# Longer DMA packets for all weights of an adaLN / cached-attention / MLP decode block, with the re-layout of the activations that they need

## The chip, the cores and the metric

The kernel runs on one core of a Trainium2 chip. Times are device microseconds (us) of one launch; a profiled execution also has a span, from its first to its last instruction, about 1.8 us shorter than the time of the same run. Engine names as in the profile: PE (TensorE), PEld (its weight loads), DVE (VectorE), ACT (ScalarE), POOL (GpSimd), SP (SyncE, which here only issues DMAs; SPq is its queue).

## The reference, cut to what matters

Two tokens (batch 2, one position each) go through one block. The weights and the caches are bf16.

```python
mod = (silu(c) @ w_mod).reshape(2, 6, 1, -1)            # w_mod 1024 x 6144
sa, ca, ga, sb, cb, gb = ...                            # its six parts
h = layernorm(x) * (1 + ca) + sa
q = h @ wq                                              # wq 1024 x 4096, 32 heads of 128
o = softmax(q k^T / sqrt(128)) v                        # caches 2 x 4 x 32768 x 128, 8 heads share one
x = x + ga * (o @ wo)                                   # wo 4096 x 1024
h = layernorm(x) * (1 + cb) + sb
x = x + gb * (gelu(layernorm(h) @ w1 + b1) @ w2 + b2)   # w1 1024 x 3584, w2 3584 x 1024
```

K and V are 134 MB, the weights 44 MB; every byte is used once. So the kernel is a long load from HBM, with everything else meant to hide under it.

## The kernel before

One ring of 160 KB per partition takes all loads. They are issued in the order of a list, each when the data that it overwrites has been used. One DMA moves 128 partitions; a run of bytes that is contiguous in HBM and in one partition becomes one packet of the profile's DMA records. What sets the packet length is therefore the layout of the source:

```python
wm_v = w_mod.rearrange("(p k) n -> p k n", k=KT8)
for k in range(KT8):                                    # 8 loads, one row of 12 KB per partition
    add(("wmod", k), [6 * DM], wm_v[:, k, :], k * 12 * KB)
for k in range(4):                                      # 2 rows of 8 KB per partition, from different places
    add(("wq", k), [2, HQ * D], A_wq[k * 256:(k + 1) * 256, :].rearrange("(k p) n -> p k n", p=128), (96 + 16 * k) * KB)
for i in range(NBG):                                    # 8 head pairs (batch x kv head)
    add_k(i, 0)                                         # 32 KB packets, ring bytes 0..32 KB
    add_k(i, 1)                                         # 32 KB packets, 32..64 KB
    add_v(i)                                            # 64 KB packets, 64..128 KB
# ... wo: 4 loads of 16 KB packets; w1: 4 loads, 7 KB; w2: 3 loads of 8 KB, then one of 6 KB, one of 2 KB
```

A matmul with such a weight contracts over the partitions, so the activation must lie on the partition on which the weight's row lies. With rows `(k p)`, partition p holds rows p, 128+p, ..., and the normed activation is already there (`inT`). One head pair is a body of the PE and DVE loop: K tiles are transposed by PE, evicted, multiplied with q; softmax; then P times V, after which V's space is free and SP issues V of the next pair.

The MLP's hidden row came out of w1 as rows, was copied to SBUF by ACT and DVE, turned to columns by 16 fp32 matmuls on PE, and got its bias on DVE.

## Time and profile before

| | before |
|---|---|
| time, median of the first 3 runs | 421.65 us (421.61 to 421.91) |
| span | 419.9 us |
| HBM read | 178.28 MB, 425 GB/s over the span |
| packets of the data queue | 8562 |
| first packet starts / last ends | 1.7 us / 416.2 us |
| PE busy / DVE / ACT | 68% / 40% / 38% |

The DMA view of the kernel before: mean busy share of the 16 DMA engines in 40 slices (tenths), what they moved, and packets, megabytes and the share of 16 engines' span that the packets took.

```profile
DMA  8999999999999999999999999999999999999995
GB/s 338 431 431 422 440 435 487 395 408 448 440 431 425 431 443 425 437 437 450 415 418 465 431 409 437 465 415 416 475 425 400 450 462 418 397 432 419 427 428 241
DMA packets 8573, 178.44 MB, mean 425 GB/s; under 512 B 873, under 2 KB 880, under 8 KB 2162
...
q1 hardware_dynamic: 8562, 178.28, 98.8%
```

Every slice but the first and the last is full. The same over stretches of the run (us of the stretch, busy us of each engine, granted PE clock, DMA share, GB/s):

```profile
0.00:4.00 4.00, 0.00 (x0) 0.00 (x0) 0.00 (x0) 1.28 (x1) 3.09 (x15) 1.00 0.59 197
4.00:60.00 56.00, 26.02 (x205) 11.34 (x205) 5.84 (x23) 2.86 (x5) 0.43 (x2) 0.90 1.02 435
60.00:345.00 285.00, 212.85 (x4307) 182.52 (x4308) 140.85 (x262) 138.17 (x232) 2.19 (x14) 0.85 1.00 433
345.00:412.00 67.00, 42.36 (x559) 27.68 (x556) 19.90 (x60) 17.02 (x32) 0.22 (x1) 0.72 1.00 425
```

The share is 1.0 from 4 us to 412 us: the kernel is bound by its DMA engines. The chain of waits gives PE half of the span, but PE only keeps pace; where the stages meet, it waits for the loads. The timeline of the kernel before (start, length, engine, line, operation, in brackets the idle time before it and what ended it):

```profile
62.96 0.82 PE L506 MATMUL psKT<-ident,K 128*128 128x128 bf16 x6 [6.37 <-DMA K<-in_A_k_cache_dram]
...
382.17 1.90 PE L616 MATMUL psS<-wo,atT 128*32 128x512 bf16 x16 [3.82 <-DMA wo<-in_A_wo_dram]
...
402.52 3.87 PE L665 MATMUL psM<-identf,S_sb 128*128 128x8 f32 x16 [1.30 <-DVE x1b L668]
...
414.06 2.88 PE L695 MATMUL psO<-gT,w 128*128 128x2 bf16 x96 [1.08 <-DMA w<-in_B_w_dram]
...
418.09 0.35 SPq L706 DMA_DIRECT2D out_dram<-c  x1
```

PE waits 6.4 us for the first K, 3.8 us for the last wo, and 1.1 us for w2 just before the end. L665 are the 16 fp32 matmuls that turn the MLP's rows to columns.

### The profile page before, as it was taken

The numbers are of one execution on the slowest core, as the hardware profiler recorded it, in microseconds if no ns is written. First come the engines' busy times: TensorE is split into PE (matmuls) and PEld (weight loads), VectorE is DVE, ScalarE is ACT, GpSimd is POOL, SyncE is SP. The second block draws the span as 40 slices with busy tenths as digits, with TensorE's granted clock in tenths as the row PEclk, the third lists the DMA queues.
The fourth block names the chain that finished last, engine by engine and source line by source line (L and its number), as shares of the span: only waits on it lengthen the run. The fifth ranks groups of instructions, "written<-read, shape, count | busy, mean of one in ns | idle before, by whom it ended". The sixth has DMA issues, their size and how long they took to land.

```text
span 419.9 us, 11452 instructions
## 1 busy us (share of the span) xinstructions
PE 285.4 (68%) x5171; PEld 225.2 (54%) x5171; DVE 167.3 (40%) x347; ACT 159.3 (38%) x269; POOL 5.9 (1%) x31
## 2 busy tenths in 40 slices
PE   1547429856892898489559928965894699264575
PEld 1105009842891497269429915962793299122244
DVE  1102006540772376157417714750674177121311
ACT  2000005552566165436526652644365166600020
POOL 3000000000000000000000000000000000000000
PEclk9999858965997799599879969985998699686566
DMA  8999999999999999999999999999999999999995
GB/s 338 431 431 422 440 435 487 395 408 448 440 431 425 431 443 425 437 437 450 415 418 465 431 409 437 465 415 416 475 425 400 450 462 418 397 432 419 427 428 241
DMA packets 8573, 178.44 MB, mean 425 GB/s; under 512 B 873, under 2 KB 880, under 8 KB 2162
## 3 DMA queue, kind: packets, MB, share of 16 engines
q1 hardware_dynamic: 8562, 178.28, 98.8%
q8 instruction: 8, 0.13, 0.1%
q14 instruction: 3, 0.02, 0.0%
HBM read 178.28 MB, written 0.00 MB: 425 GB/s over the span
## 4 chain that ended last, share of the span: by engine, by line
PE 50%; DMA 30%; ACT 11%; DVE 6%; issue 2%; SPq 1%; ACTq 0%
PE psKT L506 27%; PE psS L518 10%; DMA K<-in_A_k_cache_dram 10%; PE psO L548 9%; DMA wo<-in_A_wo_dram 9%; ACT E_sb L538 8%; DMA w<-in_B_w_dram 7%; DMA wmod<-in_w_mod_dram 4%; DVE msum L563 2%; ACT KT_sb L510 2%; DVE m1c L523 1%; ACT S_sb L522 1%; PE psM L556 1%; PE psM L534 1%; PE psM L568 1%
## 5 line engine op out<-in xcount | busy, mean ns | idle before, releaser
L506 PE MATMUL psKT<-ident,K 128*128 128x128 bf16 x2048 | 154.4, 221 | 8.0 <-DMA K<-in_A_k_cache_dram 6.4
L510 ACT ACTIVATE KT_sb<-psKT 128x1024 bf16<-128x1024 bf16 x96 | 97.7, 1025 | 127.2 <-PE psKT L506 127.2
L512 DVE COPY KT_sb<-psKT 128x1024 bf16<-128x1024 bf16 x160 | 106.2, 688 | 45.5 <-PE psKT L506 44.8
L506 PEld LDWEIGHTS psKT<-ident,K 128*128 128x128 bf16 x2048 | 118.7, 98 | 9.3 <-DMA K<-in_A_k_cache_dram 6.5
L518 PE MATMUL psS<-qcur,KT_sb 128*128 128x8 bf16 x2048 | 87.0, 167 | 0.7
L518 PEld LDWEIGHTS psS<-qcur,KT_sb 128*128 128x128 bf16 x2048 | 76.9, 96 | 1.8 <-ACT KT_sb L510 1.4
L548 PE MATMUL psO<-V,E_sb 128*32 128x512 bf16 x512 | 44.6, 526 | 0.0
L538 ACT ACTIVATE E_sb<-S_sb,negm 128x256 bf16<-128x256 f32 x64 | 32.5, 507 | 23.8 <-DVE negm L535 22.0
L556 PE MATMUL psM<-onesf,rsum 128*128 128x1 f32 x16 | 4.7, 362 | 45.4 <-DVE rsum L555 45.4
L548 PEld LDWEIGHTS psO<-V,E_sb 128*32 128x32 bf16 x512 | 16.9, 127 | 23.9 <-issue 19.5
L556 PEld LDWEIGHTS psM<-onesf,rsum 128*128 128x128 f32 x16 | 4.0, 310 | 46.1 <-DVE rsum L555 46.1
L523 DVE TENSOR_REDUCE m1c<-psS 128x8 f32<-128x512 f32 x32 | 22.2, 693 | 13.5 <-ACT S_sb L522 13.4
L522 ACT ACTIVATE S_sb<-psS 128x512 f32<-128x512 f32 x32 | 19.0, 593 | 7.7 <-PE psS L518 7.7
L561 DVE TENSOR_SCALAR msum<-psO,mk 128x128 f32<-128x128 f32 x8 | 2.8, 351 | 42.9 <-PE psO L548 42.9
L555 DVE COPY rsum<-rowsum 128x128 f32<-128x128 f32 x8 | 1.8, 226 | 41.5 <-ACT E_sb L538 41.5
L456 PE MATMUL psS<-wmod,inT 128*32 128x512 bf16 x64 | 8.4, 622 | 11.8 <-DMA wmod<-in_w_mod_dram 11.8
L568 PE MATMUL psM<-msum,hmat 128*128 128x128 f32 x16 | 3.9, 326 | 13.0 <-DVE msum L563 13.0
L477 PE MATMUL psS<-wq,inT 128*32 128x512 bf16 x64 | 7.0, 587 | 7.8 <-DMA wq<-in_A_wq_dram 6.8
L529 PE MATMUL psM<-identf,m 128*8 128x128 f32 x16 | 3.4, 296 | 13.1 <-DVE m L526 13.1
L538 ACT ACTIVATION_READ_ACCUMULATOR E_sb<-S_sb,negm 128x1 f32 x64 | 12.0, 187 | 0.0
L568 PEld LDWEIGHTS psM<-msum,hmat 128*128 128x128 f32 x16 | 2.4, 188 | 16.9 <-DVE msum L563 16.9
L427 ACT ACTIVATE stat<-stat 128x2 f32<-128x2 f32 x3 | 0.6, 204 | 28.2 <-DVE stat L426 28.2
(116 smaller groups left out, 133.3 us busy)
## 6 DMA issues: line engine op xcount, KB each, us to landing
K<-in_A_k_cache_dram SPq DMA_DIRECT2D x16, 4096.0 KB, 25.6
wmod<-in_w_mod_dram SPq DMA_DIRECT2D x8, 1536.0 KB, 16.3
wq<-in_A_wq_dram SPq DMA_DIRECT2D x4, 2048.0 KB, 37.8
wo<-in_A_wo_dram SPq DMA_DIRECT2D x4, 2048.0 KB, 34.1
w<-in_B_w_dram SPq DMA_DIRECT2D x4, 1792.0 KB, 28.9
w<-in_B_w_dram SPq DMA_DIRECT2D x3, 2048.0 KB, 30.2
w<-in_B_w_dram SPq DMA_DIRECT2D x1, 768.0 KB, 28.0
w<-in_B_w_dram SPq DMA_DIRECT2D x1, 256.0 KB, 23.8
```

The costliest lines, as they stand in the source:

```text
L456: pe(lambda e, w=it.view, k=k, ch=ch, n=n, q=q: e.matmul(bank[n][32 * q:32 * q + 32, :], lhsT=inT[:, k, :], rhs=w[:, ch * 512:(ch + 1) * 512],
L506: pe(lambda e, kq=kq, jj=jj, w=kt, t=t: e.transpose(psKT[kq][:, jj * 128:(jj + 1) * 128], w[:, t, :], ident[:, :]), reads=[it.reg, "ident" ...
L510: act(lambda e, src=src: e.activation(KT_sb[g8][:, :, :], src, ACT.Copy), reads=[f"psKT{kq}"], writes=[f"KT_sb{g8}"], sem=f"ev{cc}_{g8}")
L512: dve(lambda e, src=src: e.tensor_copy(KT_sb[g8][:, :, :], src), reads=[f"psKT{kq}"], writes=[f"KT_sb{g8}"], sem=f"ev{cc}_{g8}")
L518: pe(lambda e, t=t, jj=jj: e.matmul(ps[:, t * HPG:(t + 1) * HPG], lhsT=KT_sb[g8][:, jj, :], rhs=qcur[:, :], start=True, stop=True), reads= ...
L522: act(lambda e: e.activation(Sc, ps[:, :].rearrange("p (t h) -> p h t", h=HPG), ACT.Copy), reads=[preg], writes=[f"S_sb_{cc}"], sem=f"sc{cc}")
L523: dve(lambda e: e.tensor_reduce(m1c[:, :, cc], ps[:, :].rearrange("p (t h) -> p h t", h=HPG), AX.X, ALU.max), reads=[preg], writes=[f"m1c{ ...
L538: act(lambda e: e.activation(E_sb[:, :, h, :], S_sb[:, h, :].rearrange("p (u t) -> p u t", t=4), ACT.Exp, bias=negm[:, h:h + 1], scale=SCA ...
L548: pe(lambda e, t4=t4, tg=tg, q=q: e.matmul(psO[32 * q:32 * q + 32, :], lhsT=E_sb[:, tg // 4, :, :].rearrange("p h t -> p (h t)"), rhs=vt[: ...
L556: pe(lambda e: e.matmul(psM[:, 144:145], lhsT=rsum16.rearrange("p h e -> p (h e)"), rhs=onesf[:, 0:1], start=True, stop=True), reads=["one ...
L563: dve(lambda e, q=q: e.scalar_tensor_tensor(out=msum[:, :], in0=psO[:, q * 128:(q + 1) * 128], scalar=mk4[:, q:q + 1], in1=msum[:, :], op0 ...
L568: pe(lambda e: e.matmul(psM[:, 256:384], lhsT=hmat.rearrange("p h e -> p (h e)"), rhs=msum[:, :], start=True, stop=True), reads=["hmat", " ...
```

## The change

Fewer and longer packets for the weights: a packet has a cost of its own beside its bytes. Every weight is now cut as `(p k)`, each partition taking adjacent rows, and several rows go into one load: w_mod 2 loads of 48 KB packets (8 of 12 KB), wq 2 of 32 KB (4 of 8), wo 2 of 32 KB (4 of 16), w1 2 of 28 KB (4 of 7), w2 3 of 16 KB (8) and the same two short last loads.

The rows of wq and w1 now lie on other partitions, so the activation is moved there (`to_lines`: 8 small matmuls with a selection matrix, a multiply with a mask, a reduce). The layout of the attention's output follows wo's. The MLP's rows are turned by one DVE transpose of 32 x 32 blocks straight from PSUM; the bias enters as a first matmul.

```diff
-    for k in range(KT8):
-        add(("wmod", k), [6 * DM], wm_v[:, k, :], k * 12 * KB)
-    for k in range(4):
-        add(("wq", k), [2, HQ * D], A_wq[k * 256:(k + 1) * 256, :].rearrange("(k p) n -> p k n", p=128), (96 + 16 * k) * KB)
+    for m in range(2):
+        add(("wmod", m), [4, 6 * DM], wm_v[:, 4 * m:4 * m + 4, :], m * 48 * KB)
+    wq_v = A_wq.rearrange("(p k) n -> p k n", k=KT8)
+    for m in range(2):
+        add(("wq", m), [4, HQ * D], wq_v[:, 4 * m:4 * m + 4, :], (96 + 32 * m) * KB)
     ...
+    for m, (j0, j1, off) in enumerate(W2_ITEMS):
+        add(("w2", m), [j1 - j0, DM], w2_v[:, j0:j1, :], off * KB)
     ...
-    modulate(inT[:, :, 0:2], "inT", 0, 1)
+    modulate(hb[:, :, :], "hb", 0, 1)
+    def to_lines():
+        for k in range(KT8):
+            pe(lambda e, k=k: e.matmul(psM[:, 128 + 16 * k:144 + 16 * k], lhsT=rep[:, k, :, :].rearrange("p c u -> p (c u)"),
+                                       rhs=hb.rearrange("p k b -> p (k b)"), start=True, stop=True), ...)
+        dve(lambda e: e.tensor_tensor(pick ..., psM[:, 128:256] ..., mblk ..., ALU.mult), ...)
+        dve(red, reads=["pick"], writes=["inT"])          # reduce into inT
+    to_lines()
     ...
-    load_row("act", psS[1], "psS1", 1)
-    load_row("dve", psO, "psO", 2, 96)
-    for n, nq in ((0, 4), (1, 3)):                        # 16 fp32 matmuls, then + b1
-        ...
+    dve(lambda e: e.transpose(zrow.rearrange("p (g n c) -> p g n c", n=2, c=16), psZ[:, :, 0:448].rearrange("p n (c g) -> p g n c", g=FT)), ...)
```

## The prediction

> **What bounds it now.** The DMA engines, from the first packet to the last. The DMA view shows a mean busy share of about 1.0 in nearly every slice of the 419.9 us span. The queue's packet records: first packet at 1.7 us, last ends at 416.2 us, so 414.5 us; their durations sum to 414.5 us per engine (16 engines). No idle time is left. The chain of waits names PE for half the span, but the attention loop (about 38 us per head pair) only keeps pace with the queue and ends 8 us before the wo weights land (PE waits for the last wo load until 382.2 us). At the end PE waits for w2 at 414.1 us; about 3 us of work and the output follow the last packet.
>
> **What the change is worth.** Durations of packets in steady state, by size: 7 KB 272 ns, 8 KB 309, 12 KB 460, 16 KB 611, 32 KB 1213, 64 KB 2418. That is a line: 7.7 ns per packet plus bytes at 27.19 B/ns. The slope is the port rate in the Trainium skill, "DMA: Bandwidth & Descriptors", section "Where 436 GB/s comes from" (16 x 32 B x 850 MHz, 27.2 B/ns per engine); this trace agrees, so only the 7.7 ns can be saved. Estimate per engine from that line:
> - w_mod: 64 x 460 to 16 x 1815 ns, -0.39 us
> - wq: 64 x 309 to 16 x 1213, -0.37
> - wo: 32 x 611 to 16 x 1213, -0.14
> - w1: 64 x 272 to 16 x 1062, -0.41
> - w2: 48 x 309 to 24 x 611, -0.17; the two small last pieces stay.
>
> Sum -1.5 us, plus 12 fewer semaphore writes of 9 ns, -0.1. All of it is on the critical resource, as long as the queue never runs dry.
>
> **What it adds, off the path.**
> - c and x now queue behind 6.3 MB (14.5 us) instead of 1.6 MB: they land near 17.5 us instead of 6.8, PE starts w_mod near 21 us instead of 10. PE finishes the second half about 5 us after it lands (before 1.5); with the new turn to lines (about 1.5 us: 8 matmuls, a multiply, a reduce) q is ready near 59 us instead of 57, still before K lands near 62.
> - wo in two items: after the last lands PE has 32 matmuls, not 16 (+1.5 us; 16 took 1.9), plus the turn (+1.4): w1 starts near 396.5 instead of 394.4, needs about 6.6 us as before.
> - The MLP: two copies, 16 fp32 transposes (3.9 us) and the bias add go; one VectorE transpose of 896 columns takes their place, estimated 1.1 us from the 512-column PSUM copy (0.69 us). Activations are ready near 406 instead of 407.7.
> - Attention: only layouts of small tensors.
>
> **Prediction.** 421.65 - 1.6 = 420.05 us, range 419.0 to 421.6. Faster by over 2%: 0.01; within 2%: 0.97; slower by over 2%: 0.02.
>
> **What would show it.** Packet records: 48 KB near 1815 ns, 28 KB near 1062; sum per engine 413.0 us, last end near 414.7. Landing: K's first wait ends near 62.2 instead of 62.96. The wait of PE for w2 stays just before the end, about 1.5 us earlier. A wait for c to about 17.5 us.
>
> **What would make it wrong.** The queue running dry because a K or V load is issued late; long packets slower than the line, or their strides of 64 or 56 KB slower in HBM; the VectorE transpose taking over 4 us, or the w1 chain getting later than the last w2 piece; uneven last landings.

## The result, and the profile after

| | before | after |
|---|---|---|
| time, median of 4 runs | 421.75 us (421.61 to 421.91) | 421.61 us (421.37 to 423.05) |
| span of the profiled run | 419.9 us | 419.6 us |
| packets of the data queue | 8562 | 5428 |
| first packet starts / last ends | 1.7 / 416.2 us | 1.7 / 416.0 us |
| sum of the packets' durations, per engine | 414.5 us | 413.1 us |

The ratio is 1.0004, with a 95% interval of 0.998 to 1.0027. (A ratio is the mean time of one kernel's runs over that of the other's of the same rounds, so not quite the ratio of the medians.) The predicted gain of 1.6 us did not come; 421.61 lies just above the predicted range's upper end of 421.6. The four runs were 421.42, 421.79, 423.05 and 421.37: one is 1.3 to 1.7 us longer than the others, which the four runs of before don't show.

The DMA view of the changed kernel:

```profile
DMA  9999999999999999999999999999999999999995
...
DMA packets 5439, 178.44 MB, mean 425 GB/s; under 512 B 682, under 2 KB 690, under 8 KB 948
...
q1 hardware_dynamic: 5428, 178.28, 98.5%
```

Over a third of the packets is gone, and the rate over the span is the same 425 GB/s. The lines of the changed kernel's timeline that answer to those shown of before:

```profile
62.48 1.78 PE L531 MATMUL psKT<-ident,K 128*128 128x128 bf16 x15 [4.62 <-DMA K<-in_A_k_cache_dram]
...
382.37 3.60 PE L642 MATMUL psS<-wo,atT 128*32 128x512 bf16 x32 [6.59 <-DMA wo<-in_A_wo_dram]
...
402.40 1.12 DVE L691 STREAM_TRANSPOSE S_sb<-psZ 128x896 f32<-128x896 f32 x1 [2.94 <-PE psZ L683]
...
413.88 2.85 PE L716 MATMUL psZ<-gT,w 128*128 128x2 bf16 x96 [0.26 <-DMA w<-in_B_w_dram]
...
417.88 0.35 SPq L727 DMA_DIRECT2D out_dram<-c  x1
```

K is there 0.48 us earlier (62.48 against 62.96), the last wo 0.2 us **later** (382.37 against 382.17), w2 0.18 us earlier. So a gain arose at the start and was lost again between K and wo, where the change touches no load.

A load has landed when the last of the 16 DMA engines has landed its share. The trace keeps each engine's landing, so the mean engine and the last one can be told apart. This table is worked out from those landing records (us; end of each weight's last load, and of the last V):

```
             mean engine             last engine           first to last
             before   after  change  before   after  change  before  after
w_mod         32.07   31.95   -0.12   32.23   32.75   +0.52    0.36   1.03
wq            51.75   51.38   -0.37   53.19   52.78   -0.41    1.73   1.74
last V       361.78  361.41   -0.37  362.68  362.93   +0.25    1.72   2.37
wo           381.25  380.83   -0.42  382.12  382.33   +0.21    1.69   2.35
w1           398.53  397.85   -0.68  399.32  399.25   -0.07    1.70   2.32
w2           415.81  415.00   -0.81  416.51  416.31   -0.20    1.70   2.31
```

The mean engine gained in each weight stage and nothing in the attention, as it should; but 0.81 us in all, half of what was predicted. The last engine, for which PE waits, gained 0.20 us. These are two separate losses, and the 423.05 us run, looked into below, is a third thing.

### The profile page after: what moved, and what is told of

Same layout as the page of the kernel before. It is cut to its first block, busy times and chain, and to the rows that moved or that the text cites. A ratio compares the mean times of both kernels' runs of the same rounds, so it can differ in the third digit from the quotient of the medians.

```text
span 419.6 us, 11460 instructions
## 1 busy us (share of the span) xinstructions
PE 276.3 (66%) x5183; PEld 221.2 (53%) x5183; DVE 169.6 (40%) x351; ACT 158.8 (38%) x268; POOL 6.8 (2%) x29
## 3 DMA queue, kind: packets, MB, share of 16 engines
q1 hardware_dynamic: 5428, 178.28, 98.5%
## 4 chain that ended last, share of the span: by engine, by line
PE 56%; DMA 22%; ACT 12%; DVE 7%; issue 2%; SPq 0%; ACTq 0%
PE psKT L531 28%; PE psZ L573 10%; ACT E_sb L563 9%; DMA w<-in_B_w_dram 9%; DMA K<-in_A_k_cache_dram 9%; PE psS L543 6%; PE psZ L543 5%; DMA x<-in_A_x_dram 4%; DVE msum L588 2%; ACT KT_sb L535 2%; DVE m1c L548 1%; ACT S_sb L547 1%; PE psM L581 1%; PE psM L559 1%; PE psM L593 1%
## 5 line engine op out<-in xcount | busy, mean ns | idle before, releaser
L537 DVE COPY KT_sb<-psKT 128x1024 bf16<-128x1024 bf16 x160 | 106.3, 688 | 45.0 <-PE psKT L531 44.2
L543 PE MATMUL psS<-qcur,KT_sb 128*128 128x8 bf16 x1024 | 44.3, 166 | 2.7 <-issue 2.7
L573 PE MATMUL psZ<-V,E_sb 128*32 128x512 bf16 x512 | 44.2, 522 | 0.0
L543 PE MATMUL psZ<-qcur,KT_sb 128*128 128x8 bf16 x1024 | 42.9, 167 | 0.7
L543 PEld LDWEIGHTS psS<-qcur,KT_sb 128*128 128x128 bf16 x1024 | 39.3, 96 | 2.8 <-issue 2.8
L543 PEld LDWEIGHTS psZ<-qcur,KT_sb 128*128 128x128 bf16 x1024 | 37.8, 96 | 1.8 <-ACT KT_sb L535 1.4
L573 PEld LDWEIGHTS psZ<-V,E_sb 128*32 128x32 bf16 x512 | 16.8, 126 | 23.6 <-issue 19.1
L586 DVE TENSOR_SCALAR msum<-psZ,mk 128x128 f32<-128x128 f32 x8 | 2.8, 350 | 42.4 <-PE psZ L573 42.4
L548 DVE TENSOR_REDUCE m1c<-psZ 128x8 f32<-128x512 f32 x16 | 11.1, 693 | 10.3 <-ACT S_sb L547 10.3
L548 DVE TENSOR_REDUCE m1c<-psS 128x8 f32<-128x512 f32 x16 | 11.1, 693 | 3.2 <-ACT S_sb L547 3.1
L412 PE MATMUL psM<-ident,KT_sb 2*128 2x2 bf16 x8 | 0.6, 194 | 17.7 <-DMA KT_sb<-in_c_dram 17.7
```

The costliest lines, as they stand in the source:

```text
L537: dve(lambda e, src=src: e.tensor_copy(KT_sb[g8][:, :, :], src), reads=[f"psKT{kq}"], writes=[f"KT_sb{g8}"], sem=f"ev{cc}_{g8}")
L543: pe(lambda e, t=t, jj=jj: e.matmul(ps[:, t * HPG:(t + 1) * HPG], lhsT=KT_sb[g8][:, jj, :], rhs=qcur[:, :], start=True, stop=True), reads= ...
L548: dve(lambda e: e.tensor_reduce(m1c[:, :, cc], ps.rearrange("p (t h) -> p h t", h=HPG), AX.X, ALU.max), reads=[preg], writes=[f"m1c{cc}"])
L573: pe(lambda e, t4=t4, tg=tg, q=q: e.matmul(psO[32 * q:32 * q + 32, :], lhsT=E_sb[:, tg // 4, :, :].rearrange("p h t -> p (h t)"), rhs=vt[: ...
```

## The experiments

All eight gave correct results. The first four ran on one chip and share nine runs of before (median 421.90, 421.74 to 422.22), the second four likewise (median 422.00, 421.68 to 422.79).

### The changed kernel once more

No edit.

> The changed kernel once more. In its profile the last landing is 416.3 us against 416.5 before, although the mean landing over the 16 DMA engines of the last load moved by 0.8 us: one engine lags 2.3 us behind the first (before: 1.7). If that lag is luck of an execution, this profile shows another spread (1.5 to 2.5 us), and the runs scatter between 421.3 and 423 us. If it is built in, the spread is 2.3 us again and the runs agree within 0.3 us. Median in either case 421.4 to 421.8.

Measured: 421.43 us (422.73, 421.34, 421.20, 421.43, 421.50), ratio 0.9987 (0.9973 to 1.0001). Again one run of five is 1.2 to 1.5 us longer, and this time it is the profiled one. Its landing spread at the end is 2.83 us, so the spread is not fixed. What was not expected: the trace shows most of what made this run long. The time in which PE stood still for nothing that the profile shows ("issue"), in the window from 60 to 112 us (line, total us, times, longest), for the kernel before, for the run of the result, then for this one:

```profile
PE psKT L506 <- issue: 1.7, 1, 1.7
```

```profile
PE psS L543 <- issue: 2.7, 1, 2.7
```

```profile
PE psS L543 <- issue: 2.5, 1, 2.5
...
PE psZ L543 <- issue: 1.4, 1, 1.4
```

In this run PE stops twice in the first pass of its loop, 3.9 us in all. V of the second head pair, which waits until PE has used V of the first, is then issued later. SP's issues, first in the run of the result, then here:

```profile
73.88 14.90 SPq L385 DMA_DIRECT2D K<-in_A_k_cache_dram  x2
104.83 0.33 SPq L385 DMA_DIRECT2D V<-in_A_v_cache_dram  x1
```

```profile
74.81 16.23 SPq L385 DMA_DIRECT2D K<-in_A_k_cache_dram  x2
107.12 0.33 SPq L385 DMA_DIRECT2D V<-in_A_v_cache_dram  x1
```

In this run the first packets of that V start at 109.0 us, and most of the first 16 take longer than the usual 2418 ns, one by 1.8 us, as the first packets of the whole program do: the queue had run empty and had to start anew. From the mean landing of K before it to that of this V it takes 19.98 us here and 19.31 us in the run of the result: 0.67 us lost. (Before: 19.31.) That is not the whole of it: the last landing of w2 is 1.24 us later than in the run of the result (417.56 against 416.31), of which the mean engine accounts for 0.76 us (415.77 against 415.00) and the wider spread for the rest.

### Small first packets

```diff
+WMOD_ITEMS = ((0, 1), (1, 4), (4, 8))
-    for m in range(2):
-        add(("wmod", m), [4, 6 * DM], wm_v[:, 4 * m:4 * m + 4, :], m * 48 * KB)
+    for m, (k0, k1) in enumerate(WMOD_ITEMS):
+        add(("wmod", m), [k1 - k0, 6 * DM], wm_v[:, k0:k1, :], k0 * 12 * KB)
```

> The changed kernel, but w_mod arrives as 12 KB, 36 KB and 48 KB packets, so that the first packets are small as in the kernel before. Theory L (late engine): the first 48 KB packets of the changed kernel start one engine 1.05 us late, and that engine, later hit by an instruction fetch (1.4 us), ends last; with a small first packet the spread after w_mod is about 0.4 us and the time falls by about 0.6 us, to about 421.0. Rival (only the size of the per-packet cost was wrong, the start does not matter): no change, 421.6 (8 more packets per engine cost 0.04 us).

Measured: 421.49 us (423.42, 421.01, 421.49, 422.42, 421.02). As it stands this is inconclusive: the median falls neither with the theory nor clearly with the rival, since two runs of five are of the long kind. The spread after w_mod is 0.46 us, as theory L said. The profiled run is the longest, 423.42, and again ran dry: PE stopped for 1.60 and 2.95 us, V of the second pair was issued at 109.47 us, and the DMA share fell by up to half (us of the stretch, busy us by engine, clock, DMA share, GB/s; a packet counts where it starts):

```profile
107.00:108.00 1.00, 1.00 (x16) 0.46 (x12) 0.00 (x0) 0.00 (x0) 0.00 (x0) 0.50 0.76 328
108.00:109.00 1.00, 1.00 (x20) 0.37 (x12) 0.00 (x0) 0.00 (x0) 0.00 (x0) 0.74 0.70 295
109.00:110.00 1.00, 0.42 (x8) 0.00 (x0) 0.49 (x2) 0.00 (x0) 0.00 (x0) 1.00 0.46 197
```

From K's mean landing to this V's it takes 20.89 us, 1.57 us more than in the run of the result. The three short runs (421.01, 421.02, 421.49) suggested that the start does matter; the question is asked again below, without dry queues.

### K and V in packets of 16 KB

The order of the keys within a head pair is free as long as K and V agree, so their packets can be shortened without any other change:

```diff
-  A_k_cache[i % 2, i // 2].rearrange("(p h c t) d -> h p c (t d)", h=2, c=2, p=128)[hf]
+  A_k_cache[i % 2, i // 2].rearrange("(h c p t) d -> h p c (t d)", h=2, c=2, p=128)[hf]
-  A_v_cache[i % 2, i // 2].rearrange("(p c t) d -> p c (t d)", c=NCH, p=128)
+  A_v_cache[i % 2, i // 2].rearrange("(c p t) d -> p c (t d)", c=4, p=128)
```

> The changed kernel with K and V in 16 KB packets instead of 32 and 64 KB: 320 more packets per engine, same bytes, same result. Theory P (a packet costs 5.1 ns: the 7.7 ns of the records less the 2.6 ns by which packets of one engine overlap): +1.6 us, 423.2. Rival R (7.7 ns, as predicted; the gain was lost elsewhere): +2.5 us, 424.1. Rival Z (large packets cost nothing at all): 421.6.

Measured: 422.93 us (422.70 to 423.09, five runs). Against 421.43 that is 1.50 us for 320 packets per engine, 4.7 ns each. Theory P, which said 5.1 ns, is close, if a little high; the 7.7 ns of the prediction, and packets that cost nothing, both fall. No run is of the long kind, although the DMA is slower, and PE's longest stop in the first pass is 0.3 us:

```profile
PE psS L543 <- issue: 0.3, 1, 0.3
```

### K and V in packets of 4 KB

The same with `c=8` for K and `c=16` for V (and the ring's view split in four to take them).

> The same with 4 KB packets: 1856 more packets per engine than in the changed kernel. Theory P: +9.5 us, 431.1. Rival R: +14.3 us, 435.9. Rival Z: 421.6. Records of one 4 KB packet about 158 ns in all theories.

Measured: 430.31 us (430.06 to 430.38). 8.88 us for 1856 packets per engine, 4.8 ns each, with the same answer at nearly six times the number. The record of one 4 KB packet reads 159 ns, as all theories said. But from one head pair to the next the mean landing of V advances 39.79 us (mean of seven steps), against 38.70 in the changed kernel: 1.10 us for 232 packets, again 4.7 ns. The difference to 7.7 ns is, for the most part, overlap: in the packet records of all ten traces, a packet starts 3 to 4 ns before the recorded end that lies nearest to its start (median; 2.6 ns is the mean in before), which is taken to be that of the packet before it on its engine. Adding up recorded durations counts that overlap twice.

### K and V of the first head pair alone in 16 KB packets

```diff
-  ....rearrange("(p h c t) d -> h p c (t d)", ...)
+  ....rearrange("(h c p t) d -> h p c (t d)" if i == 0 else "(p h c t) d -> h p c (t d)", ...)
-  ....rearrange("(p c t) d -> p c (t d)", ...)
+  ....rearrange("(c p t) d -> p c (t d)" if i == 0 else "(p c t) d -> p c (t d)", ...)
```

> The changed kernel with K and V of the first of the eight head pairs alone in 16 KB packets (40 more packets per engine, about +0.2 us at 4.8 ns each). Theory F (PE stops in the first pass of its loop because its instruction fetch waits behind long data packets; V of the second pair is then issued late, in some executions after the queue has run dry): the stop near 76 to 87 us (2.75 us in the changed kernel, 3.9 and 4.5 us in two dry executions) is gone as in the run with all of K and V in 16 KB, V of the second pair is issued near 101 us, no execution runs dry, so all runs lie within 0.4 us of each other, at 421.3 to 421.7. Rival S (the runs over 422.4 are scatter of the chip): the runs over 422.4 stay, 1 or 2 in 5.

Measured: 421.47 us, and all five runs within 421.37 to 421.62. PE's stop is 0.6 us instead of 2.7, V of the second pair is issued at 102.92 us instead of 104.83 or 107.12:

```profile
PE psS L543 <- issue: 0.6, 1, 0.6
```

```profile
74.67 11.45 SPq L385 DMA_DIRECT2D K<-in_A_k_cache_dram  x2
102.92 0.33 SPq L385 DMA_DIRECT2D V<-in_A_v_cache_dram  x1
```

The long runs are gone: 0 of 15 when the two kernels below that have the same edit on the changed kernel are counted with this one, where the changed kernel and its small-start version had 4 of 14. Four long runs out of 29 would all fall into those 14 by chance about once in 24 times. The 15 also ran on another chip, on which the changed kernel itself was not run; but on the chip of the first four experiments the two kernels with all of K and V in short packets had no long run in 9, and the two without had 3 in 10. Theory F holds in what it says of the cure: shorter data packets in the first pass shorten PE's stop and keep the queue fed. Two details of the expectation failed: the stop was shortened, not gone, and V was issued at 102.92 us, not near 101.

The traces also tie PE's stop to its instructions. Each holds 8 packets of 16384 B on the instruction queue. Here is the first matmul after each stop in the kernel before, in the run of the result, in the changed kernel once more (two stops) and in this run:

```profile
82.67 0.38 PE L506 MATMUL psKT<-ident,K 128*128 128x128 bf16 x4 [1.65 <-issue]
```

```profile
83.15 0.24 PE L543 MATMUL psS<-qcur,KT_sb 128*128 128x8 bf16 x4 [2.75 <-issue]
```

```profile
77.57 0.22 PE L543 MATMUL psZ<-qcur,KT_sb 128*128 128x8 bf16 x3 [1.39 <-issue]
...
85.38 0.24 PE L543 MATMUL psS<-qcur,KT_sb 128*128 128x8 bf16 x4 [2.51 <-issue]
```

```profile
81.81 0.24 PE L543 MATMUL psS<-qcur,KT_sb 128*128 128x8 bf16 x4 [0.61 <-issue]
```

In the packet records of the same traces an instruction packet ends at 81.40, at 81.74, at 76.28 and 83.98, and at 80.50 us. So each stop ends 1.3 to 1.4 us after such a packet; over all seven traces with a stop of over 0.4 us it is 1.2 to 1.4 us, nine times out of nine. And these blocks come further apart beside long data packets: from the third to the fourth it takes 6.0 to 6.6 us in the six traces with 16 or 4 KB packets in the first pass, 7.1 to 9.7 us in the four with 32 and 64 KB. That PE waits for its instructions there is thus well supported; that the fetch itself stands behind data packets is inferred from the spacing.

### The same, with small first packets as well

> The same plus the small first w_mod packets. Theory F and L: 421.0 to 421.3 in every run, faster than e5 by 0.3 us; spread of the 16 engines after w_mod 0.45 us instead of about 1.0. If the late start of one engine does not matter: equal to e5.

Measured: 421.17 us (421.03 to 421.25), 0.30 us less than without the small first packets, and the two sets of runs do not overlap. The mean engine ends its last load at the same time (415.28 against 415.29 us); the last engine ends 0.42 us earlier (415.93 against 416.35), since the spread is 1.58 us instead of 2.02. After w_mod it is 0.51 instead of 0.81. This is theory L by itself: same packets to within 8 per engine, same mean, and the time follows the last engine. All ten traces agree with it: the five kernels that start with 48 KB packets have a spread of 0.67 to 1.04 us after w_mod and 2.02 to 2.83 at the end, the five that start with 12 KB packets 0.36 to 0.51 and 1.58 to 1.84.

### The kernel before, with K and V of its first head pair in 16 KB packets

The edit of the experiment before last, on the kernel before.

> The kernel before with K and V of the first head pair in 16 KB packets. Its queue was never seen to run dry (13 runs within 0.6 us), so theory F expects the PE stop of 1.65 us at 81 us to go and the time to rise by the 40 packets only: 421.9 + 0.2 = 422.1. If the stop itself costs time: about 1.6 us faster, 420.3. Against e5 it gives the value of the change without dry queues: 184 packets x 4.8 ns = 0.9 us if every engine gains alike, 0.2 to 0.5 if the last engine gains less.

Measured: 422.06 us (421.93 to 422.15), ratio to before 1.0001 (0.9988 to 1.0015). The stop of PE (1.7 us in before) shrank to 1.1 us and the time did not fall: while the queue is full, PE's stop costs nothing that these runs show, though only 0.5 us of it was taken away. With this pair the value of the change can be read without dry queues: 421.47 against 422.06, **-0.59 us**, with no overlap between the runs. The mean engine ends its last load 0.80 us earlier (415.29 against 416.09), the last engine 0.50 us earlier (416.35 against 416.85).

### w_mod as before, the rest of the change kept, first head pair in 16 KB

`WMOD_ITEMS` has eight entries of one row each.

> The changed kernel with w_mod as in the kernel before (8 loads of 12 KB packets), K and V of the first pair in 16 KB. 48 packets per engine more than e5: +0.23 us by their cost; by theory L the last engine is 0.6 us less behind. Sum about 0.3 us faster than e5. If the start is unimportant: 0.2 us slower than e5.

Measured: 421.37 us (421.23 to 421.42), 0.10 us faster by the median than with w_mod in 48 KB packets, not 0.3, and the two sets of runs overlap (421.37 to 421.62). Its sign is theory L's, its size was off: the spread after w_mod is 0.44 instead of 0.81 us, but at the end 1.75 instead of 2.02, so the last engine won back 0.27 us, not 0.6, against the 48 more packets. Long packets for w_mod, from the first byte on, thus brought nothing. Beside 421.17 for 12, 36 and 48 KB this is 0.20 us slower, with 40 packets per engine more; the mean engine ends 0.13 us later (415.41 against 415.28), and the rest is spread.

## Why the prediction was right or wrong

What it said of the bound holds. The kernel is bound by its DMA engines before and after. The records it foretold came: 48 KB packets took 1815 ns, 28 KB packets 1062 ns, the sum per engine 413.1 us (predicted 413.0). The price of the re-layout is off the path: c landed at 17.7 us (17.5), q's last copy ended at 58.4 us, 4.1 us before K; w1 started at 397.5 us (396.5), the DVE transpose took 1.12 us (1.1), and PE still waits for w2 before the end, though by 0.26 us only. The Trainium skill, "VectorE: DVE Perf Modes", section "The three transpose paths", says that DVE transposes 32 x 32 blocks only; that is what this layout was made for. No trace shows the blocks; they show that one instruction of 1.12 us replaced 3.87 us of PE work and two copies.

It failed in these steps.

1. **"a line: 7.7 ns per packet plus bytes at 27.19 B/ns ... only the 7.7 ns can be saved".** This is the term of the sum that was mis-sized. A packet costs 4.7 to 4.8 ns, measured by adding 320 and 1856 packets per engine. 184 fewer packets are then worth 0.88 us, an estimate from that figure, not 1.5; the mean engine measured -0.81 us (-0.80 with the first pair cured). The prediction took recorded durations as if they followed each other; they overlap by 3 to 4 ns (median). It was also misled by a check that seemed to close: durations of before sum to 414.5 us, exactly the time from the first packet to the last. That agreement was an accident of errors that nearly cancel. By an estimate from the records of before, overlap makes the sum about 1.2 us too long (480 packets of 2 KB or more per engine, 2.6 ns each on average); on the other side the sum leaves out the semaphore packets (0.5 us per engine) and the instruction packets (0.5), and the last engine lands 0.7 us after the mean one.

2. **"sum per engine 413.0 us, last end near 414.7".** The sum is an average over 16 engines, but a load is there when the last engine is. The risk was named ("uneven last landings") and given no size. The first 48 KB packets of the run took up to 3001 ns, so one engine was 1.03 us late after w_mod, where 12 KB packets had left all within 0.36. Later fetches of instructions add lags of about 1.4 us to single engines (worked out in the last section), and by the end the spread was 2.31 us against 1.70. So of 0.81 us the last engine kept 0.20 in the profiled run. With the first pair cured it kept 0.50 of 0.80, and 0.92 us with small first packets too (415.93 against 416.85).

3. **"as long as the queue never runs dry".** 4 of 14 runs of the changed kernel and its small-start version were long; the two of them that were profiled were dry near 109 us, and lost 0.67 and 1.57 us there (the other two left no trace). The prediction named the risk ("a K or V load is issued late") but gave it no size and no place; it came at the turn from the first to the second pair. The link is PE's stop in the first pass of its loop: 1.7 us in before, 2.7 in the changed kernel, 3.9 and 4.5 in the two dry runs. Shorter K and V packets in that pass shorten it, to 0.6 us at most, and no run with them was long.

What stays open: why the changed kernel stops longer in the first pass than the kernel before, though K's and V's packets are the same. Its PE program is some instructions longer ahead of the loop, which may shift where the blocks of instructions begin; the second block comes at 61.87 us instead of 67.07, so they did shift, but that this is the reason is argued, not tested. One of 22 runs of before took 422.79 us, without a profile, so before may run dry too, only more rarely. And in no trace is the lag of one DMA engine followed through the whole run by that engine's number, which the records do not have; which lags met on one engine is inferred from the sorted landings.

The best version is the change with w_mod in 12, 36 and 48 KB packets and the first head pair in 16 KB: 421.17 us, ratio to before 0.998 (0.9966 to 0.9994), with runs within 0.22 us. It beats the kernel before by 0.2%. The changed kernel as it stands did not run beside it; with the first pair alone in 16 KB it took 421.47.

## What to carry to other kernels

Price a packet (or any pipelined unit) by the distance from start to start, or better by adding a few hundred of them on the chip, not by its recorded duration; and judge a load by its last engine, not by a sum over 16. When a kernel is bound by its DMA engines as this one is, a longer packet saves nanoseconds (here 4.7 to 4.8), and the first long packets of a stream can cost more in uneven starts than they save, so start with a short one. Instruction fetches share the DMA engines with the data: in the first pass of a loop, an engine beside long data packets can stop for microseconds (here 1.7 to 4.5), which matters when a buffer is freed by that pass.

## What the Trainium skill lacked or had wrong

- "DMA: Bandwidth & Descriptors", section "Where 436 GB/s comes from", has the port rate as 16 x 32 B x 850 MHz. The slope of packet durations is 27.19 B/ns per engine, and whole stretches ran at 433 to 435 GB/s, from HBM. The same page's specifications give an HBM limit of about 358 GB/s per core, and that section says without a condition that the HBM side binds for HBM to SBUF; with one core running it did not. The page's own table of bandwidths, made with one core, has 425, so only that sentence lacks its condition.
- The same page, "Why small descriptors are slow (HBM only)", speaks of a fixed overhead of about 3 cycles per packet and judges packets worth joining only at 256 B or less. It has no figure for long packets. Here a packet cost 4.7 to 4.8 ns, measured between 4 and 64 KB: 3% of a 4 KB packet, 0.4% of a 32 KB one. Three cycles at the 850 MHz of the point above would be 3.5 ns, an estimate from the page, nearer to that than the prediction's 7.7 ns.
- "Runtime: NRT & Kernel Launch", section "Instruction fetch mechanics", says that instructions come in blocks of 16 KiB by a DMA queue of the sequencer's own, and calls the cost mostly hidden. The records agree on the block: 8 packets of 16384 B on the instruction queue in each trace, each 0.9 us long, and each followed by one data packet that took about 0.5 us longer than usual (0.3 where it had 4 KB), so about 1.4 us of lag for one DMA engine. They disagree on hidden: PE stopped for 1.7 to 4.5 us in the first pass of its loop, 1.1 us at most when the data packets there were 16 KB. The section warns of a stall at a taken branch, but these stops, at 76 to 87 us, come before the loop's first branch (106.3 us in the kernel before, 106.5 in the changed one).
- "DMA: Bandwidth & Descriptors", section "Queues, rings and completion order", says that a DMA engine changes between queues only after a whole packet, where its packet is a group of descriptors, not surely one record of the profile. That fits the longer stop beside 64 KB packets (2418 ns each) and the instruction blocks that come 7.1 to 9.7 us apart there, not 6.0 to 6.6. But the page does not warn that long data packets hold up instruction fetches, and no record here shows a fetch waiting by itself.
- No page says that the first packets after an empty queue are slower and uneven: in the run of the result the first 48 KB packet of each engine took 2.2 to 3.0 us instead of 1.8, and the 16 engines were up to 1.05 us apart afterwards and stayed so through w_mod.
